# Attention maxima 22 steps ahead instead of 24, and the softmax shift sent in rows instead of half rows

## The chip, the cores and the metric

The kernel runs on one core of one Trainium2 chip. A core has five engines with a queue of their own each: TensorE (PE in the profile; its weight loads stand as PEld), VectorE (DVE), ScalarE (ACT), GpSimd (POOL), and SyncE (SP), which here only issues transfers. They meet through semaphores. The metric is the device time of one execution in microseconds; lower is better.

## The reference

One transformer block with conditioned layer norms, on 2048 tokens of width 512:

```python
mod = silu(c) @ w_mod                       # 512 -> 6 x 512: sa, ca, ga, sb, cb, gb
h = layernorm(x) * (1 + ca) + sa
# A: attention, 32 heads of 16
q, k, v = split(h @ wqkv)
p = softmax(q @ k.T * 16 ** -0.5)           # 2048 x 2048 for each head
x = x + ga * ((p @ v) @ wo)
h = layernorm(x) * (1 + cb) + sb
# B: spatial shift, then an MLP 512 -> 1792 -> 512
x1 = h + shifted(gelu(layernorm(h) @ w1)) @ w2
x = x + gb * (x1 + gelu(layernorm(x1) @ w3) @ w4)
```

All inputs are float32. The weights are scaled up (by 8 in attention, by 64 in B), so the scores reach far and the softmax needs its maximum taken off.

## The kernel before, in words

**Precision.** A float32 product is made of three TensorE products of parts (a high and a low part on each side). For the scores this is folded into the contraction: each of the 16 dimensions of a head takes three rows, so queries and keys of a head stand in 48 of 64 rows. Two heads lie in one tile, head j = 0 in partitions 0 to 63 and j = 1 in 64 to 127; TensorE works on both halves at the same time.

**Units and steps.** Attention is cut into 64 units: 4 chunks of 512 queries times 16 pairs of heads. A unit has 16 steps, one for each 128 keys, 1024 steps in all. In a step each of the two heads has

- a score product (`sc`, L1009): 128 keys x 512 queries into one of seven shared PSUM banks; the weights are a block of the keys `kst`, the streamed operand is the query tile `qtl`;
- an exponential on ScalarE (`pt<-sc`, L1005), written as a 32-bit integer; its upper half is used as a 16-bit number as it stands, the lower half after one halving (`pt<-pt`), which the planner puts on GpSimd (L1058) or, where GpSimd is behind, on ScalarE (L153 in the profile, the same operation);
- value products (`pv`, L1083 for the upper and L1080 for the lower halves).

**The maximum.** A softmax shift for each query is needed before the first score of its unit. It is found by a second product with the roles turned (`mb`, L993): the weights are 128 queries out of 512, the streamed operand 512 keys. VectorE takes the maximum along the keys (`mx<-mb`, L989). A unit needs 4 query groups x 4 key chunks x 2 heads = 32 such products, as many as it has scores. They run `LEAD` steps ahead: beside the scores of step s stand the maxima products of step s + LEAD. Before the first score lie LEAD steps with maxima alone, and in the last LEAD steps there are scores alone.

**The shift.** When a unit's last maximum is in, `max_fin` makes from it a high and a low part in `nm` (two small ScalarE operations L1040 and L1041, one on GpSimd L1042), one value for each query: queries lie along the partitions there. They must become two rows of the query tile (rows 62 and 63 of each head's half, against rows of ones in the keys), so that the score product itself subtracts them. `shift_rows` does that with transfers from SBUF to SBUF on SP's queue: one for each head, part and half of the 512 queries, eight in a unit, each of 128 pieces of 8 bytes (two neighbouring queries from one partition). The first score of the unit waits for them. A group of 128 queries must therefore be the queries that lie in one column of `nm`: groups 0 and 1 are the even and odd queries of the first 256, groups 2 and 3 those of the last 256, and the maxima product's weights are read from the query tile with a step of two.

**Loads.** Keys and queries of a unit come from DRAM by four transfers (`load_unit`) into one of three buffers, issued 32 steps ahead of its first score, when the unit three before has ended.

**The order of work.** A planner (`Sched`) writes all queues at build time from modelled durations: it keeps a clock for each engine and places operations of chains when their engine is modelled free. The attention loop goes in blocks of three rows (a row is one head's score and the other head's maxima product, which use different halves of TensorE), then the value products of an earlier block. Between blocks the generators' work is filled in: the projections of q, k and v during the first units, the beginning of the tail (`tail(0)`: wo, w1) during the last 30 steps. After attention the tail runs for the last 500 us, most of it products L356, L358, L360.

Of the kernel before, what the change touches and what calls it, by code (L numbers as in the profile page):

```python
# [8 lines left out]
F32 = mybir.dt.float32  # L9
# [25 lines left out]
VMAX = 2.0 ** 14  # L35
VD = 20

LEAD = 24
LAG = 2
CARRY = 3000.0  # L40
BMAX = 1600.0
# [286 lines left out]
def kernel(ctx, tc, A_x, A_wqkv, A_wo, B_w1, B_w2, B_w3, B_w4, c, w_mod, out):  # L328
    nc = tc.nc
    te, act, dve, pool, dma = nc.tensor, nc.scalar, nc.vector, nc.gpsimd, nc.sync  # L330
# [21 lines left out]
    def mark(key):  # L352
        return None, 0, lambda: done.add(key)
# [64 lines left out]
    sch = Sched()  # L418
# [535 lines left out]
    qst, vst, mxs = {}, {}, {}  # L954
# [18 lines left out]
    def bank(nm):  # L973
        x = sm.take()
        return x, ap_.tile([P, CH], F32, name=nm, tag=f"s{x}", bufs=1)

    def max_part(m, j):

        u, i = divmod(m, 16)
        c, g = divmod(i, 4)  # L980
        if u not in mxs:
            mxs[u] = at.tile([P, 2, 4, NC], F32, name="mx", tag="mx", bufs=2)
        x, b = bank("mb")
        ready, sm.t[x] = sm.t[x], LATE
        r = slice(64 * j, 64 * j + 62)
        lhs = qst[u][r, (g // 2) * 256:(g // 2 + 1) * 256].rearrange("p (n l) -> p l n", l=2)[:, g % 2]

        def after(e):
            end = sch.crit("D", 605, e + PX, lambda: dve.reduce_max(mxs[u][:, j, g, c:c + 1], b, axis=AX.X))  # L989
            sm.t[x] = end + XP["D"]  # L990
            if (c, g, j) == (NC - 1, 3, 0):
                max_fin(u)
        return ready, lambda: te.matmul(b, lhs, kst[u % 3][r, c * CH:(c + 1) * CH], start=True, stop=True), after  # L993

    def score_part(s, j):

        u, kt = divmod(s, NKT)
        if j == 0:
            pt[s] = at.tile([P, 2, CH], I32, name="pt", tag="pt", bufs=NPT)
        x, b = bank("sc")  # L1000
        ready, sm.t[x] = sm.t[x], LATE
        r = slice(64 * j, 64 * j + 64)

        def after(e):
            ea = sch.crit("A", 480, e + PX, lambda: act.activation(pt[s][:, j], b, AF.Exp))  # L1005
            sm.t[x] = ea + XP["A"]
            if j:
                e_exp[s] = e_hi[s] = ea
        return ready, lambda: te.matmul(b, kst[u % 3][r, kt * P:(kt + 1) * P], qst[u][r], start=True, stop=True), after  # L1009

    def row_pair(s, j):

        parts = []
        if 0 <= s < NS:
            parts.append((j, score_part(s, j)))
        if s + LEAD < NS:
            parts.append((1 - j, max_part(s + LEAD, 1 - j)))
        parts = [x for _, x in sorted(parts, key=lambda x: x[0])]

        def mms():  # L1020
            for _, mm, _ in parts:
                mm()
        e = sch.put("P", CROW, max(x[0] for x in parts), mms)
        return [partial(x[2], e) for x in parts]

    def max_fin(u):
        mf = at.tile([P, 8], F32, name="mf", tag="mf", bufs=2)
        nm = at.tile([P, 2, 8], F32R, name="nm", tag="nm", bufs=2)
        mx = mxs.pop(u)

        def shift_rows():
            for j in range(2):
                for i in range(2):
                    r = 64 * j + 62 + i
                    for h in range(2):
                        sch.dma(dma.dma_start,
                                qst[u][r:r + 1, h * 256:(h + 1) * 256].bitcast(F32).rearrange("o (p l) -> o p l", l=2),
                                nm[:, i, 4 * j + 2 * h:4 * j + 2 * h + 2].bitcast(F32))
        sch.chain(("D", 85, lambda: dve.reduce_max(mf.rearrange("p (j g) -> p j g", j=2), mx, axis=AX.X)),
                  ("A", 100, lambda: act.activation(mf, mf, AF.Copy, scale=-1.0, bias=PEXP)),  # L1040
                  ("A", 100, lambda: act.activation(nm[:, 0], mf, AF.Copy)),  # L1041
                  ("G", 250, lambda: pool.tensor_tensor(nm[:, 1], mf, nm[:, 0], op=OP.subtract)),  # L1042
                  (None, 0, shift_rows), mark(("shift", u)), prio=0, ready=sch.T["D"])
# [550 lines left out]

    blocks = [list(range(i, min(i + GRP, 2 * NS))) for i in range(-2 * LEAD, 2 * NS, GRP)]
    pvs = [x for s in range(0, NS, 2) for x in ((s, 0), (s + 1, 0), (s, 1))]
    due = 0.0
    for k, blk in enumerate(blocks + [[]] * (LAG + CPER)):
# [18 lines left out]
        t, start = CIN, 0.0  # L1617
        need = sum((s >= 0) + (s + LEAD < NS) for s, _ in row)
        sch.flush(need)
        banks = sorted(sm.t)  # L1620
        n = 0
        for s, i in row:
            n += (s >= 0) + (s + LEAD < NS)

# [102 lines left out]
```

## Time and profile before

| what | us |
|---|---|
| median of 3 runs (lowest to highest) | 2027.61 (2023.54 to 2027.86) |
| the profiled execution | 2030.02 |
| its span, first to last instruction | 2028.2 |
| PE busy / PEld busy | 1941.1 / 1168.8 |
| DVE busy / ACT busy / POOL busy | 1658.8 / 1511.4 / 1569.9 |
| maxima alone (first maxima product to first score) | 95.5 to 130.4 |
| scores and maxima together | 130.4 to 1488.4 |
| scores alone | 1488.4 to 1528.9 |

The profiled execution is 2.4 us above the median of the runs shown, and 1.8 us of it lie outside the span. An engine's busy time is the union of its instructions. On TensorE the ends are modelled, and the shown time of a product includes its weight load where that was not hidden: 0.50 us against 0.39. In a timeline row, "x2 0.30" are two overlapping instructions of one kind that together took 0.30 us; the brackets behind a row give the idle time ahead of it and what ended it. The chain is the sequence of work that ended last, followed back through whoever released each step.

### The profile page before, as it was taken

What the parts mean: (1) busy time and instruction counts of PE and PEld (TensorE: products, weight loads), DVE (VectorE), ACT (ScalarE), POOL (GpSimd) and SP (SyncE); (2) the same over time, 40 slices, a digit from 0 to 9 for tenths busy, and PEclk for the clock granted to TensorE, in tenths of its full rate; (3) what the DMA queues carried; (4) which work ended last, traced back from release to release, by engine and by line L of the source; (5) the groups of instructions that cost most, each with busy time, mean ns of one, the idle gap of its engine ahead of it and who ended that gap; (6) DMA issues with size and microseconds to landing.
All of it is one profiled execution on the core that took longest, in us unless ns stands there. A gap on an engine that the chain in (4) does not pass through costs nothing.

```text
span 2028.2 us, 41674 instructions
## 1 busy us (share of the span) xinstructions
PE 1941.1 (96%) x14456; PEld 1168.8 (58%) x14456; DVE 1658.8 (82%) x2979; ACT 1511.4 (75%) x3085; POOL 1569.9 (77%) x1488
## 2 busy tenths in 40 slices
PE   8999999999999999999999999999998889999999
PEld 5755554554444444444444444444447778898998
DVE  6398788879999999999999999999965786556443
ACT  6438887768999989999999999999984554344443
POOL 6349998879999999999999999999994554335222
PEclk9989999999999999999999999999999899999999
DMA  8877666544443435353434343454414677553541
GB/s 302 233 203 183 158 190 165 135 126 118 81 97 81 97 72 106 72 107 72 107 72 98 80 102 76 95 162 93 90 38 146 228 261 274 218 201 122 200 154 68
DMA packets 185508, 278.01 MB, mean 137 GB/s; under 512 B 117104, under 2 KB 127856, under 8 KB 169008
## 3 DMA queue, kind: packets, MB, share of 16 engines
q1 hardware_dynamic: 181792, 267.20, 49.0%
q10 hardware_dynamic: 2304, 4.20, 0.6%
q0 software_dynamic: 1200, 3.93, 0.5%
q8 instruction: 115, 1.88, 0.4%
q14 instruction: 97, 0.79, 0.1%
HBM read 211.81 MB, written 62.91 MB: 135 GB/s over the span
## 4 chain that ended last, share of the span: by engine, by line
PE 61%; DVE 16%; ACT 10%; issue 6%; POOL 4%; DMA 3%; SPq 1%; ACTq 0%; POOLq 0%; DVEq 0%
PE mb L993 13%; DVE mx L989 11%; PE pv L1083 9%; PE sc L1009 8%; ACT pt L1005 7%; PE w L360 6%; PE w L356 6%; PE w L358 6%; PE pv L1080 4%; PE ot L1110 3%; POOL pt L1058 2%; PE xT L1244 1%; DMA wr<-Ws 1%; DMA wst<-in_A_wqkv_dram 1%; SPq L132 1%
## 5 line engine op out<-in xcount | busy, mean ns | idle before, releaser
L989 DVE TENSOR_REDUCE mx<-mb 128x1 f32<-128x512 f32 x2048 | 1250.1, 680 | 74.5 <-PE mb L993 68.6
L1058 POOL TENSOR_SCALAR pt<-pt 128x1024 f16<-128x1024 uint16 x953 | 1248.1, 1365 | 78.7 <-ACT pt L1005 75.7
L1005 ACT ACTIVATE pt<-sc 128x512 int32<-128x512 f32 x2048 | 1061.3, 615 | 125.6 <-PE mb L993 98.0
L993 PE MATMUL mb<-kst,qtl 62*128 62x512 f32 x2048 | 782.7, 462 | 19.9 <-ACT pt L1005 9.9
L1009 PE MATMUL sc<-qtl,kst 64*128 64x512 f32 x2048 | 739.7, 449 | 5.0 <-DVE mx L989 2.5
L993 PEld LDWEIGHTS mb<-kst,qtl 62*128 62x128 f32 x2048 | 360.1, 193 | 232.3 <-ACT pt L1005 159.9
L1009 PEld LDWEIGHTS sc<-qtl,kst 64*128 64x128 f32 x2048 | 337.0, 186 | 186.8 <-DVE mx L989 119.3
L1083 PE MATMUL pv<-pt,vst 128*32 128x512 f16 x4096 | 385.3, 397 | 20.5 <-ACT ac L1100 20.5
L1456 POOL TENSOR_TENSOR g<-sq,g 128x256 fp32r<-128x256 f32 (+1 forms) x124 | 97.2, 787 | 200.6 <-ACT g L1455 187.2
L1080 PE MATMUL pv<-pt,vst 128*32 128x512 f16 (+1 forms) x2048 | 220.8, 389 | 2.5 <-POOL pt L1058 2.4
L1083 PEld LDWEIGHTS <-vst 128*32 128x32 bf16 x4096 | 91.8, 93 | 227.7 <-issue 209.2
L358 PE MATMUL w<-A,wr 128*128 128x256 f32 (+1 forms) x520 | 156.1, 300 | 0.3 <-DVE A L346 0.3
L356 PE MATMUL w<-A,wr 128*128 128x256 f32 (+1 forms) x520 | 155.9, 300 | 0.2 <-ACT A L350 0.2
L360 PE MATMUL w<-A,wr 128*128 128x256 f32 (+1 forms) x520 | 155.8, 300 | 0.0
L1452 ACT ACTIVATE sq<-w 128x256 f32<-128x256 f32 (+1 forms) x130 | 52.3, 402 | 136.0 <-PE w L360 127.2
L356 PE MATMUL w<-wr,g 128*128 128x512 f32 x270 | 106.9, 396 | 2.9 <-DMA wr<-Ws 2.9
L360 PE MATMUL w<-wr,g 128*128 128x512 f32 x270 | 106.5, 394 | 0.9 <-POOL g L1456 0.9
L358 PE MATMUL w<-wr,g 128*128 128x512 f32 x270 | 106.1, 393 | 0.0
L1434 DVE SCALAR_TENSOR_TENSOR sq<-sq,w 128x256 f32<-128x256 f32 (+1 forms) x130 | 58.3, 449 | 57.7 <-ACT sq L1454 57.5
L356 PEld LDWEIGHTS w<-A,wr 128*128 128x128 f32 x520 | 101.7, 196 | 1.6 <-ACT A L350 0.5
L358 PEld LDWEIGHTS w<-A,wr 128*128 128x128 f32 x520 | 101.5, 195 | 1.5 <-DVE A L346 0.5
L360 PEld LDWEIGHTS w<-A,wr 128*128 128x128 f32 x520 | 101.3, 195 | 0.5 <-issue 0.5
(156 smaller groups left out, 2128.5 us busy)
## 6 DMA issues: line engine op xcount, KB each, us to landing
wr<-Ws SPq DMA_DIRECT2D x66, 1024.0 KB, 5.5
vst<-Vs SPq DMA_DIRECT2D x64, 768.0 KB, 5.6
kst<-Ks SPq DMA_DIRECT2D x126, 384.0 KB, 6.2
Ws<-wr SPq DMA_DIRECT2D x14, 1024.0 KB, 6.2
qtl<-Qs SPq DMA_DIRECT2D x128, 96.0 KB, 4.3
Vs<-vt SPq DMA_DIRECT2D x32, 384.0 KB, 4.2
Ks<-qk SPq DMA_DIRECT2D x16, 512.0 KB, 4.2
Qs<-qk SPq DMA_DIRECT2D x16, 512.0 KB, 3.0
```

What stands on the lines that cost most here:

```text
L356: te.matmul(o, lh, rh, start=first, stop=False)
L358: te.matmul(o, lh, rl, start=False, stop=False)
L360: te.matmul(o, ll, rh, start=False, stop=last)
L989: end = sch.crit("D", 605, e + PX, lambda: dve.reduce_max(mxs[u][:, j, g, c:c + 1], b, axis=AX.X))
L993: return ready, lambda: te.matmul(b, lhs, kst[u % 3][r, c * CH:(c + 1) * CH], start=True, stop=True), after
L1005: ea = sch.crit("A", 480, e + PX, lambda: act.activation(pt[s][:, j], b, AF.Exp))
L1009: return ready, lambda: te.matmul(b, kst[u % 3][r, kt * P:(kt + 1) * P], qst[u][r], start=True, stop=True), after
L1058: e_low[s] = XP["G"] + sch.crit("G", 1345, ready, lambda: pool.tensor_scalar(o, i, 0.5, 1.0, op0=OP.mult, op1=OP.mult))
L1080: te.matmul(acc[r:r + n, :], v[:, kt + i, c:c + n].bitcast(F16), pt[s + i].bitcast(F16)[:, j, 0::2], start=False, stop=kt == NKT - 2, skip ...
L1083: te.matmul(acc[r:r + 32, :], v[:, kt, r:r + 32], pt[s].bitcast(F16)[:, j, 1::2], start=kt == 0, stop=False, skip_group_check=True)
L1110: te.matmul(b[:, t * n:(t + 1) * n], ac[:, t * P:(t + 1) * P], smat.rearrange("p j d -> p (j d)"), start=True, stop=True)
L1456: ("G", cG(n), lambda: pool.tensor_tensor(lo, sq, hi, op=OP.subtract)), (None, 0, end), bank=b)
```

## The change

`LEAD` goes from 24 to 22. The shift's rows go in one transfer each, four in a unit instead of eight, each of 128 pieces of 16 bytes (four neighbouring queries from one partition). The groups of queries follow: group g is now every fourth query from g on, and the maxima product's weights are read from the query tile with a step of four, 16 bytes, instead of two.

```diff
-LEAD = 24
+LEAD = 22
@@ max_part
         r = slice(64 * j, 64 * j + 62)
-        lhs = qst[u][r, (g // 2) * 256:(g // 2 + 1) * 256].rearrange("p (n l) -> p l n", l=2)[:, g % 2]
+        lhs = qst[u][r, :].rearrange("p (n l) -> p l n", l=4)[:, g]
@@ max_fin, shift_rows
             for j in range(2):
                 for i in range(2):
                     r = 64 * j + 62 + i
-                    for h in range(2):
-                        sch.dma(dma.dma_start,
-                                qst[u][r:r + 1, h * 256:(h + 1) * 256].bitcast(F32).rearrange("o (p l) -> o p l", l=2),
-                                nm[:, i, 4 * j + 2 * h:4 * j + 2 * h + 2].bitcast(F32))
+                    sch.dma(dma.dma_start, qst[u][r:r + 1, :].bitcast(F32).rearrange("o (p l) -> o p l", l=4),
+                            nm[:, i, 4 * j:4 * j + 4].bitcast(F32))
```

Since the planner writes the queues, LEAD moves more than the maxima. No instruction is added but for the transfers, of which there are 256 instead of 512. Of the halvings of `pt`, 82 instead of 71 stand on ScalarE and 942 instead of 953 on GpSimd. Of the projections' products, 64 instead of 72 stand between the first maxima product and the first score, and 14 of the tail's (3 of wo, 11 of w1) that stood among the last scores now stand behind the last one.

On TensorE, around the program's first score (`mb` maxima products, `sc` scores, `q` and `vb` projection work; the numbers behind `kst` and `qtl` tell buffers apart), the queue before reads:

```order
L993 MATMUL mb<-kst_967,qtl_965 128x512 x3
L356 MATMUL q<-hT_118,wp 128x512
L358 MATMUL q<-hT_118,wp 128x512
L360 MATMUL q<-hT_118,wp 128x512
L356 MATMUL q<-hT_118,wp 128x512
L358 MATMUL q<-hT_118,wp 128x512
L1009 MATMUL sc<-qtl_145,kst_147 128x512
L993 MATMUL mb<-kst_967,qtl_965 128x512 x2
L1009 MATMUL sc<-qtl_145,kst_147 128x512 x2
L993 MATMUL mb<-kst_967,qtl_965 128x512
```

The same place in the changed program:

```order
L803 MATMUL vb<-wab,gcol 128x256
L993 MATMUL mb<-kst_967,qtl_965 128x512 x3
L803 MATMUL vb<-wab,gcol 128x256 x3
L993 MATMUL mb<-kst_967,qtl_965 128x512 x5
L1009 MATMUL sc<-qtl_145,kst_147 128x512
L993 MATMUL mb<-kst_967,qtl_965 128x512
L356 MATMUL q<-hT_118,wp 128x512
L358 MATMUL q<-hT_118,wp 128x512
L360 MATMUL q<-hT_118,wp 128x512
```

The first score comes four maxima products earlier, inside a block of three rows instead of at its start, and the q products that stood ahead of it now follow.

On ScalarE, around the shift of the unit 46 (`mf` and `nm` are the shift, `pt<-sc` the exponentials, L153 a halving, L1100 the copy at the end of a unit), before:

```order
L1005 ACTIVATE pt<-sc 128x512 x6
L153 ACTIVATE pt<-pt 128x1024
L1005 ACTIVATE pt<-sc 128x512 x3
L1040 ACTIVATE mf<-mf 128x8
L1041 ACTIVATE nm<-mf 128x8
L1005 ACTIVATE pt<-sc 128x512 x21
L153 ACTIVATE pt<-pt 128x1024
L1100 ACTIVATE ac<-pv 128x512
```

In the changed program (its line numbers are two lower from here on):

```order
L1005 ACTIVATE pt<-sc 128x512 x6
L153 ACTIVATE pt<-pt 128x1024
L1005 ACTIVATE pt<-sc 128x512 x3
L1038 ACTIVATE mf<-mf 128x8
L1039 ACTIVATE nm<-mf 128x8
L1005 ACTIVATE pt<-sc 128x512 x18
L1098 ACTIVATE ac<-pv 128x512
L1005 ACTIVATE pt<-sc 128x512 x3
L153 ACTIVATE pt<-pt 128x1024
```

Of the exponentials behind `nm`, 12 belonged to the unit at work before the first one of the unit 46 came; now 8 do. Over the attention's regular part it is 12 to 14 before and 7 to 10 now: the shift is made two steps, four scores, nearer to its use.

## The prediction

> **What bounds the kernel now.** I read the page first: span, busy times and the chain.
>
> ```profile
> span 2028.2 us, 41674 instructions
> PE 1941.1 (96%) x14456; PEld 1168.8 (58%) x14456; DVE 1658.8 (82%) x2979; ACT 1511.4 (75%) x3085; POOL 1569.9 (77%) x1488
> PE mb L993 13%; DVE mx L989 11%; PE pv L1083 9%; PE sc L1009 8%; ACT pt L1005 7%; PE w L360 6%; PE w L356 6%; PE w L358 6%; PE pv L1080 4%; PE ot L1110 3%; POOL pt L1058 2%; PE xT L1244 1%; DMA wr<-Ws 1%; DMA wst<-in_A_wqkv_dram 1%; SPq L132 1%
> ```
>
> PE seems to bound all, but a modelled busy time says little, and the costliest single entries of the chain are the maxima products and their reductions, the work the change touches. So I cut the span into stages with the windows view (us, then busy and count of PE, PEld, DVE, ACT, POOL, then granted clock): maxima alone, projections beside attention, regular attention, scores alone. The same view, for the reductions of L989 alone, counts the steps.
>
> ```profile
> 95.00:130.00 35.00, 33.49 (x123) 19.91 (x124) 33.60 (x59) 5.33 (x12) 9.22 (x8) 0.90 0.68 169
> 130.00:500.00 370.00, 359.06 (x2768) 191.67 (x2767) 313.21 (x535) 296.78 (x613) 329.48 (x281) 0.99 0.63 162
> 500.00:1488.00 988.00, 955.85 (x8119) 453.58 (x8118) 944.41 (x1642) 909.92 (x1803) 942.56 (x805) 0.99 0.43 91
> 1488.00:1529.00 41.00, 38.82 (x275) 20.17 (x273) 19.00 (x38) 29.25 (x59) 39.82 (x43) 1.00 0.26 74
> ...
> 500.00:1488.00 988.00, 937.90 (x1543) 0.99 0.43 91
> ```
>
> Maxima alone are bound by DVE (33.6 of 35), scores alone by POOL (39.8 of 41). In the long regular stage, half the span, PE, DVE and POOL are all at 95 to 97%: nothing there is spare by more than 5%. Two reductions a step give 988 / (1543 / 2) = 1.28 us a step.
>
> Where three engines are level, the chain tells which one a small extra lands on. I took it for 25 regular us (share by line; then the first and the last of the 15 pieces that start with an exposed weight load, those of 0.42 us and more; 10 of the 15 are `mb`, 5 are `sc`):
>
> ```profile
> by line: PE mb L993 26.8%; ACT pt L1005 20.1%; PE pv L1083 18.3%; PE sc L1009 16.0%; issue 8.7%; PE pv L1080 6.4%; PE ot L1110 4.0%; ACT mf L1040 0.9%; ACT pt L153 0.5%; ACTq L1041 0.3%; ACT nm L1041 0.1%; ACTq L1005 0.0%
> ...
> 1126.11 0.49 PE mb L993
> 1126.61 0.23 PE sc L1009
> ...
> 1149.07 0.74 PE mb L993 x2
> ```
>
> A product behind another takes 0.23 us, one behind a wait 0.42 to 0.50, since its weight load then stands in the path.
>
> **The change part by part. First, the weights with a step of four.** It adds no instruction; it changes how 2048 loads walk through the query tile. These are their groups, then one block of three rows in the order of time:
>
> ```profile
> L993 PEld LDWEIGHTS mb<-kst,qtl 62*128 62x128 f32 x2048 | 360.1, 193 | 232.3 <-ACT pt L1005 159.9 <-DVE mx L989 40.3 <-issue 5.0
> L1009 PEld LDWEIGHTS sc<-qtl,kst 64*128 64x128 f32 x2048 | 337.0, 186 | 186.8 <-DVE mx L989 119.3 <-ACT pt L1005 32.5 <-issue 12.0
> ...
> L993 PEld LDWEIGHTS mb<-kst,qtl x2048: 189/191/335, 95.5 to 1488.4; 62*128 62x128 f32 x187
> ...
> 1128.31 0.18 PEld L1009 LDWEIGHTS sc<-qtl,kst 64*128 64x128 f32 x1 [0.45 <-DVE mx L989]
> 1128.31 0.30 PEld L993 LDWEIGHTS mb<-kst,qtl 62*128 62x128 f32 x2
> 1128.43 0.41 PEld L1009 LDWEIGHTS sc<-qtl,kst 64*128 64x128 f32 x2
> ```
>
> Two loads that overlap take 0.30 us, one alone 0.19, so the pass over 128 weights takes 0.11 and the rest is latency. In that pass an `sc` load (contiguous) walks over 128 x 4 = 512 bytes of each partition, an `mb` load (step two) over 1024 bytes, that is 9.3 bytes per ns. A streamed operand of 512 contiguous numbers, 2048 bytes in 0.23 us, goes at 8.9. No row of this trace goes faster. With a step of four the load walks over 2048 bytes; at the same pace it takes 0.22 us, 0.11 more. The bounds: nothing, since the step from one to two, 186 to 193 ns, shows no kink; and 335 - 191 = 0.14, the longest load seen. I take 0.11, because the streamed operand is the nearest row in bytes walked and it stands at the limit.
>
> The Trainium skill says on this ("SBUF — State Buffer", Specifications (TRN2)) that a 16-byte line of SBUF has to be hit at least twice for full bandwidth. Two hits, the step of two, run at full pace here, as it says; one hit no run here shows, and the page gives no figure for it; by it the load costs more, as taken.
>
> What lies on the path: loads of the second and third row of a block are issued while the products ahead still stream, and 0.22 still fits under 0.23, so these cost nothing; if a load took longer than 0.23, that cover would be gone for all 2048. The exposed ones are the first of each run of rows. In the 25 us above, 26.8% and 16.0% are 10.7 us with 10 exposed `mb` loads. Over the span the chain has 13% and 8%, 426 us, so 426 / 10.7 x 10 = 398 exposed `mb` loads: 398 x 0.11 = 44 us. Upper end: the 5 of 15 that start with `sc` are slowed as well, since the `mb` beside them starts later and the rows end together: 597 x 0.14 = 84 us. Lower end: 0. The other engines cover little: at 95% busy they are 44 us short of filling the stage themselves. Queued behind a slow load are the block's scores and value products; VectorE and ScalarE wait for them.
>
> **Second, LEAD 22.** Two steps of maxima alone go: -2 x 35.0 / 24 = -2.9 us. Two steps more have both: +2 x 1.28 = +2.6. Two steps of scores alone go: -2 x 41.0 / 24 = -3.4. But those ends were also filled with other products, and the queues in order show where they went: 8 q products into the projection stage (PE 359 of 370) and 14 of the tail behind the last score. At the 0.23 us of a 512-wide product (the 11 of w1 are 256 wide, half of that) it is 8 x 0.23 + 3 x 0.23 + 11 x 0.12 = 3.8 us that come back. Sum 0.1. Counted by PE alone, the program has four rows fewer, -4 x 0.23 = -0.9, and one or two changes between rows and value products. I take -1, with -4 (the moved products find holes) and +4 as ends.
>
> **Third, the shift in four transfers.** The rows for all transfers of it, and for the unit 46:
>
> ```profile
> L132 SPq DMA_DIRECT2D qtl<-nm x512: 468/593/1826, 121.3 to 1496.7; - x171
> ...
> DMA to landing us min/median/max: 1.9/2.0/5.9
> ...
> qtl<-Qs SPq DMA_DIRECT2D x128, 96.0 KB, 4.3
> ...
> 1140.90 5.29 SPq L132 DMA_DIRECT2D qtl<-nm  x8
> 1147.61 0.31 SPq L132 DMA_DIRECT2D qtl<-Qs  x1
> ...
> 1147.08 0.50 PE L1009 MATMUL sc<-qtl,kst 64*128 64x512 f32 x1
> 1147.43 0.61 PE L1009 MATMUL sc<-qtl,kst 64*128 64x512 f32 x2
> ```
>
> Today there is almost nothing to spare: the eighth issue starts at about 1140.90 + 5.29 - 0.60 = 1145.6 and lands 1.9 us later, at 1147.5; the scores that need it start at 1147.08 (first head) and 1147.43. The shift is now made 2 x 1.28 = 2.56 us nearer to the scores. Four issues fewer, 5.29 / 2, give 2.6 back. An issue costs by its pieces, 128 before and after, and not by bytes: the query load in the same rows moves 96 KB, in 48 long pieces, with a 0.31 us issue. So 0, as good as exact; the lower end is 0, since PE hardly waits for it now, the upper one issue of the longest kind (1826 - 593 = 1.2 us) in every third of 63 units: 25 us. Behind the shift on SP stand the loads of the next unit; they are first used two steps later than now, so they gain room.
>
> **Fourth, 11 halvings from POOL to ACT.** 1.37 us each on either (POOL 1.365 in its group, 1.37 the one at 1137.75 on ACT), 15 us off POOL's 943 and onto ACT's 910 of 988: both have room, cost 0, ends -2 and +2.
>
> ```profile
> L1058 POOL TENSOR_SCALAR pt<-pt 128x1024 f16<-128x1024 uint16 x953 | 1248.1, 1365 | 78.7 <-ACT pt L1005 75.7
> 1137.75 1.37 ACT L153 ACTIVATE pt<-pt 128x1024 f16<-128x1024 uint16 x1
> ```
>
> **Sum.** 2030.0 (the profiled execution) + 44 - 1 + 0 + 0 = 2073; against the median, 2.4 lower, 2070.6, so 2070 us.
>
> **The rivals.**
> - The load isn't dearer, and the rest cancels: 2027.6 - 1, within 4 us, so 2027. For it speaks that 186 to 193 shows no kink. It decides whether the `mb` load's mean stays near 193. The same page of the Trainium skill, in its section on the DMA port swizzle, also says that fp32 can be stepped over by four for free; that reading gives this time.
> - Faster: the load isn't dearer, and the moved products fall into holes of PE. In the stage of scores alone, whose chain is POOL's at 65%, two steps less shorten POOL's own queue and one halving of 1.4 us there moves to ACT: -2.9 + 2.6 - 3.4 - 1.4 = -5.1, so 2022.5. It decides from the point where less than 1 us of the 3.8 comes back.
>
> ```profile
> by line: POOL pt L1058 64.8%; POOL trs L1353 8.3%; issue 7.5%; DVE A L346 3.1%; DVE mx L989 2.9%; POOL trs L1357 2.3%; ACT A L350 1.5%; POOL trs L1358 1.4%; PE w L356 1.2%; PE w L358 1.1%; PE wo L356 1.0%; PE sc L1009 1.0%; PE pv L1080 1.0%
> ```
>
> - The shift lands late, the load is not dearer: `nm` waits behind halvings on ACT and POOL (the one at 1137.75 stands just ahead of it), and with two steps less a wait of 0.5 us at each of 62 units gives +31: 2058. Against it: the halved number of issues.
> - The load takes more than the 0.23 us that cover it, say 0.33: then each of 2048 rows takes 0.1 more, +205, less what PE idles before such loads and could give (232 and 187 us in the groups, mostly while it waits for its own consumers): some +150, 2180. Nothing in the trace shows so slow a load.
>
> **How the numbers follow.** Forecast 0.53, no change 0.14, faster 0.18, late shift 0.10, uncovered load 0.05. What a measurement here can tell from no change is about 0.2%, 4 us. Slower by more: 0.53 + 0.10 + 0.05 = 0.68; within: 0.14; faster: 0.18. The forecast's own range is 2040 to 2095: half the exposed loads at 0.06, up to 600 at 0.11. The range for all reaches from the middle of the faster case, 2021, to 2096; it leaves out the uncovered load, half of the faster case and the forecast's far end.
>
> **What would show it.** The `mb` weight loads at about 300 ns instead of 193, those of `sc` still at 186; the first `mb` product of a block at 0.60 instead of 0.50; a step of 1.33 us or more in the regular stage, DVE and POOL below 93% there, and more of the chain on `mb`. Of the shift: 256 issues of some 0.59 us, landing in 2.0, no wait of `sc` for them beyond today's. The stage of maxima alone near 32 us. The prediction is wrong if the loads stay near 193, or if they rise and the regular stage doesn't lengthen, which would mean that exposed loads were hidden by the waits for DVE and ACT that they follow.

## The result and the profile after

| | before | changed |
|---|---|---|
| median, us | 2026.4 (2023.54 to 2027.86, 4 runs) | 2056.5 (2053.49 to 2057.77, 4 runs) |
| ratio, 95% interval | | 1.0146 (1.0133 to 1.016) |
| profiled execution / its span | 2030.02 / 2028.2 | 2053.49 / 2051.7 |

The changed kernel is slower by 1.46%, some 30 us; the profiled spans differ by 23.5 us, since the profiled execution of the changed kernel is the fastest of its four and that of before (2030.02) lies above the four listed here. The page of the changed kernel, span, engines and chain, and last the chain by engine of before:

```profile
span 2051.7 us, 41094 instructions
PE 1996.3 (97%) x14456; PEld 1314.7 (64%) x14456; DVE 1663.5 (81%) x2979; ACT 1526.0 (74%) x3096; POOL 1560.1 (76%) x1477
PE 82%; DVE 8%; ACT 4%; issue 2%; POOL 1%; DMA 1%; ACTq 0%; SPq 0%; DVEq 0%; POOLq 0%
PE mb L993 20%; PE sc L1009 14%; PE pv L1081 14%; PE pv L1078 6%; PE w L360 5%; PE w L358 5%; PE w L356 5%; DVE mx L989 4%; PE ot L1108 3%; ACT pt L1005 3%; PE xT L1242 1%; PE q L356 1%; DVE tst L367 1%; PE v L356 1%; PE q L360 1%
...
PE 61%; DVE 16%; ACT 10%; issue 6%; POOL 4%; DMA 3%; SPq 1%; ACTq 0%; POOLq 0%; DVEq 0%
```

The chain went over to PE: 82% of the span instead of 61%, the maxima products `mb` 20% instead of 13%, VectorE 8% instead of 16%. PE is busy 55 us longer (1941.1 before), on the same products. The groups say which (the first line is the group of `mb` products before), and one block in the order of time shows how (weight loads first, then the products; the number ahead of the engine is the duration):

```profile
L993 PE MATMUL mb<-kst,qtl 62*128 62x512 f32 x2048 | 782.7, 462 | 19.9 <-ACT pt L1005 9.9
...
L993 PE MATMUL mb<-kst,qtl 62*128 62x512 f32 x2048 | 846.9, 521 | 9.3 <-ACT pt L1005 4.9
L993 PEld LDWEIGHTS mb<-kst,qtl 62*128 62x128 f32 x2048 | 520.1, 307 | 177.0 <-ACT pt L1005 120.5
L1009 PEld LDWEIGHTS sc<-qtl,kst 64*128 64x128 f32 x2048 | 369.0, 191 | 160.6 <-DVE mx L989 107.4
...
1125.01 0.31 PEld L993 LDWEIGHTS mb<-kst,qtl 62*128 62x128 f32 x1 [0.45 <-ACT pt L1005]
1125.01 0.18 PEld L1009 LDWEIGHTS sc<-qtl,kst 64*128 64x128 f32 x1
...
1125.01 0.62 PE L993 MATMUL mb<-kst,qtl 62*128 62x512 f32 x1
1125.01 0.50 PE L1009 MATMUL sc<-qtl,kst 64*128 64x512 f32 x1
1125.35 0.40 PE L993 MATMUL mb<-kst,qtl 62*128 62x512 f32 x1
```

The `mb` load takes 307 ns instead of 193; the `sc` load is unchanged at the head of a block (0.18), its mean goes from 186 to 191. The first `mb` product of the block takes 0.62 us instead of 0.50, the next, whose load ran under it, 0.40.

Where in the span the time went, I read from stages whose edges are the first scores of units 0, 16 and 60 and the end of the last score. In the regular part, units 16 to 59 (windows view: us, PE, PEld, DVE, ACT, POOL), before and after:

```profile
533.90:1435.70 901.80, 872.48 (x7398) 413.03 (x7395) 861.89 (x1499) 831.16 (x1645) 860.97 (x735) 0.99 0.44 93
```

```profile
553.10:1460.40 907.30, 904.08 (x7394) 510.06 (x7390) 864.59 (x1496) 839.39 (x1651) 852.27 (x726) 1.00 0.41 92
```

PE's busy time rises by 31.6 us there and its idle time falls from 29.3 to 3.2: the stage is only 5.5 us longer, and PE has nothing left in it. The other stages: up to the first score 126.8 instead of 130.4 us (-3.6); units 0 to 15 426.3 instead of 403.5 (+22.8); from unit 60 to the last score 92.9 instead of 93.7; the tail 498.4 instead of 498.8. The sum is the 23.5 us, nearly all of it in units 0 to 15, where the projections run.

The shift arrives in time, as its transfers show (tile `nm`: duration min, median, max in ns; then who waited):

```profile
L132 SPq DMA_DIRECT2D qtl<-nm x256: 468/588/1560, 121.7 to 1523.3; - x128
...
who waited for it (us, times):
  POOL nm L1040: 15.3, 12
  PE sc L1009: 0.6, 2
```

### The profile page after: what moved, and what is told of

It reads as the page before. It is cut to its first block, busy times and chain, and to the rows that moved or that the text cites. A ratio compares the mean times of both kernels' runs of the same rounds, so it can differ in the third digit from the quotient of the medians.

```text
span 2051.7 us, 41094 instructions
## 1 busy us (share of the span) xinstructions
PE 1996.3 (97%) x14456; PEld 1314.7 (64%) x14456; DVE 1663.5 (81%) x2979; ACT 1526.0 (74%) x3096; POOL 1560.1 (76%) x1477
## 4 chain that ended last, share of the span: by engine, by line
PE 82%; DVE 8%; ACT 4%; issue 2%; POOL 1%; DMA 1%; ACTq 0%; SPq 0%; DVEq 0%; POOLq 0%
PE mb L993 20%; PE sc L1009 14%; PE pv L1081 14%; PE pv L1078 6%; PE w L360 5%; PE w L358 5%; PE w L356 5%; DVE mx L989 4%; PE ot L1108 3%; ACT pt L1005 3%; PE xT L1242 1%; PE q L356 1%; DVE tst L367 1%; PE v L356 1%; PE q L360 1%
## 5 line engine op out<-in xcount | busy, mean ns | idle before, releaser
L993 PE MATMUL mb<-kst,qtl 62*128 62x512 f32 x2048 | 846.9, 521 | 9.3 <-ACT pt L1005 4.9
L993 PEld LDWEIGHTS mb<-kst,qtl 62*128 62x128 f32 x2048 | 520.1, 307 | 177.0 <-ACT pt L1005 120.5
L1009 PEld LDWEIGHTS sc<-qtl,kst 64*128 64x128 f32 x2048 | 369.0, 191 | 160.6 <-DVE mx L989 107.4
L153 ACT ACTIVATE pt<-pt 128x1024 f16<-128x1024 uint16 x82 | 114.0, 1390 | 0.0
L356 PEld LDWEIGHTS w<-A,wr 128*128 128x128 f32 x520 | 101.4, 195 | 1.1 <-ACT A L350 0.2
L358 PEld LDWEIGHTS w<-A,wr 128*128 128x128 f32 x520 | 101.0, 194 | 1.4 <-DVE A L346 0.4
```

The source lines that it names most:

```text
L153: fn()
L356: te.matmul(o, lh, rh, start=first, stop=False)
L358: te.matmul(o, lh, rl, start=False, stop=False)
```

## The experiments

Three theories stand against each other: the slower weight load costs the time; the new order (LEAD and what it moves) does; the shift lands late.

**One part alone: the step of four.** The kernel before, with eight transfers; each puts its pairs where the new grouping wants them.

```diff
@@ max_part
-        lhs = qst[u][r, (g // 2) * 256:(g // 2 + 1) * 256].rearrange("p (n l) -> p l n", l=2)[:, g % 2]
+        lhs = qst[u][r, :].rearrange("p (n l) -> p l n", l=4)[:, g]
@@ shift_rows
-                                qst[u][r:r + 1, h * 256:(h + 1) * 256].bitcast(F32).rearrange("o (p l) -> o p l", l=2),
+                                qst[u][r:r + 1, :].bitcast(F32).rearrange("o (p a l) -> o p a l", a=2, l=2)[:, :, h],
```

> LEAD 24 and eight transfers as before; only the maxima weights are read with a step of four, and each transfer's pieces land where that grouping wants them. Theory of the weight load: the whole loss is here, the mb load at 306 ns as in the changed kernel and a ratio to before of 1.012 to 1.018. Theory of the order (LEAD and the new queues cost the time): the load rises too, but the ratio stays within 1.003. Theory of a late shift: as the theory of the order, since the shift has its old lead here.

Measured: 2058.19 us, ratio 1.0153 (1.0134 to 1.0173). The weight load alone makes the whole loss. `mb` products take 521 ns in the mean, as in the changed kernel.

```profile
PE 1986.1 (97%) x14456; PEld 1314.7 (64%) x14456; DVE 1661.7 (81%) x2979; ACT 1515.4 (74%) x3085; POOL 1572.9 (76%) x1488
...
L993 PEld LDWEIGHTS mb<-kst,qtl 62*128 62x128 f32 x2048 | 520.0, 307 | 175.8 <-ACT pt L1005 126.4 <-DVE mx L989 23.3 <-issue 7.1
```

PE is busy 45.0 us longer than before; the span, 2057.5 us, is 29.3 longer; PE's idle time (span less busy) falls from 87.1 to 71.4. By stages: units 0 to 15 +10.4 us, units 16 to 59 +18.8, the rest +0.1.

**The changed kernel with the old LEAD.**

```diff
-LEAD = 22
+LEAD = 24
```

> The changed kernel with LEAD back at 24: step of four, four transfers. Theory of the weight load: 1.012 to 1.018 against before, within 0.3% of the changed kernel, since LEAD is worth -1 us and at most 4. Theory of the order: near 1.000. Theory of a late shift: under 1.005, the shift now having 2.5 us to spare.

Measured: 2060.28 us, ratio 1.0165 (1.0139 to 1.019). LEAD doesn't cost the time, and with four transfers the loss is the same as with the eight of the first experiment. Whether it brings some can't be told from these intervals. Its small sum hides larger parts. Against this kernel's profile (first score at 130.6, units 0 to 15 414.4 us, units 16 to 59 918.8), the changed one's stages are -3.8, +11.9 and -11.5.

**LEAD alone: the kernel before with 22, the shift in eight transfers.**

```diff
-LEAD = 24
+LEAD = 22
```

> LEAD 22 alone: step of two and eight transfers as before. By the reckoning of the shift, it is made 2.56 us nearer to its score and nothing is saved at its transfers, with 0.1 to 0.6 us to spare before: some 2 to 2.5 us late at each of about 47 regular units, so +90 to +120 us if PE's wait goes through, ratio 1.04 to 1.06, and waits of sc for the transfers of nm of that size in the profile. Rival: the other engines catch up behind the wait or the planner's order hides it, under 1.01.

Measured: 2132.13 us, ratio 1.0514 (1.049 to 1.0539). The wait is there, first line of PE's waits, and the page's chain by engine and by line:

```profile
PE sc L1009 <- DMA qtl<-nm: 66.2, 55, 1.9
...
PE 57%; ACT 8%; DVE 8%; SPq 7%; issue 7%; POOL 6%; DMA 6%; ACTq 0%; POOLq 0%; DVEq 0%
PE mb L993 10%; PE sc L1009 9%; PE pv L1083 8%; SPq L132 7%; ACT pt L1005 6%; PE w L360 5%; PE w L356 5%; PE w L358 5%; POOL pt L1058 5%; DMA qtl<-nm 5%; DVE mx L989 4%; PE pv L1080 3%; PE ot L1110 2%; PE xT L1244 1%; PE q L356 1%
```

55 waits of up to 1.9 us; the transfers and SP's issuing of them hold 12% of the chain (7 for SP, its other issues on that line among them, and 5 for the transfers), where before only SP's 1% appears. But the waits make 66.2 us, 1.2 us each, and not the whole 104. Over the span PE's idle time grows by 54.7 us and its busy time by 48.4, with the granted clock at 0.966 instead of 0.987. Units 16 to 59 and, below, a stretch 0.9 us behind the end of one such wait (in the last columns the granted clock, DMA share and GB/s):

```profile
548.70:1534.50 985.80, 913.06 (x7394) 420.86 (x7393) 869.99 (x1497) 845.05 (x1651) 856.84 (x726) 0.95 0.40 85
...
619.90:623.30 3.40, 3.40 (x22) 1.67 (x16) 1.89 (x3) 1.73 (x4) 2.31 (x3) 0.50 1.14 202
```

The stage is 84.0 us longer than before and PE is busy 40.6 us longer in it on the same products, at a clock of 0.95 instead of 0.99. The trace has 24 stretches at half the clock there, 88.7 us together; before has 2, 10.2 us. Half of the difference, an estimate, is 39 us. Of the 24 stretches 22 begin during a wait for the shift or within 2 us after it; that the waits bring the lower clock is likely from this, but no run takes the two apart. So two steps of lead are worth 100 us with eight transfers, waits and clock together, and the change can only take them away because it halves the transfers at the same time.

**Half the loads.** In the kernel before, the step of four for the first head of each pair alone.

```diff
@@ max_part
+        if j == 0:
+            lhs = qst[u][r, :].rearrange("p (n l) -> p l n", l=4)[:, g]
+        else:
             lhs = qst[u][r, (g // 2) * 256:(g // 2 + 1) * 256].rearrange("p (n l) -> p l n", l=2)[:, g % 2]
@@ shift_rows
-                                qst[u][r:r + 1, h * 256:(h + 1) * 256].bitcast(F32).rearrange("o (p l) -> o p l", l=2),
+                                (qst[u][r:r + 1, :].bitcast(F32).rearrange("o (p a l) -> o p a l", a=2, l=2)[:, :, h] if j == 0 else qst[u][r:r + 1, h * 256:(h + 1) * 256].bitcast(F32).rearrange("o (p l) -> o p l", l=2)),
```

> As before, but the step of four for the first head's maxima products alone, 1024 of 2048 loads. Theory of exposed loads that add up: half the loss of the full step, ratio 1.006 to 1.009. Rival, a loss only where the slow load is the last thing the block waits for: far from half, under 1.003 or near the full 1.014.

Measured: 2047.15 us, ratio 1.0102 (1.0081 to 1.0123): 18.5 us of the full step's 29.5. That is between half and two thirds, above the 1.006 to 1.009 that was expected, though the intervals still allow the half. Neither form of the rival (under 1.003, or near the full loss) holds.

**VectorE as the bound.** Two of a unit's 32 reductions are done twice (the result is the same), first in the kernel before, then in that of the first experiment.

```diff
-            end = sch.crit("D", 605, e + PX, lambda: dve.reduce_max(mxs[u][:, j, g, c:c + 1], b, axis=AX.X))
+            def maxima():
+                for _ in range(1 + (g == 0 and j == 0 and c < 2)):
+                    dve.reduce_max(mxs[u][:, j, g, c:c + 1], b, axis=AX.X)
+            end = sch.crit("D", 605 * (1 + (g == 0 and j == 0 and c < 2)), e + PX, maxima)
```

> The kernel before, with 2 of a unit's 32 reductions done twice (the planner knows of it): 1.2 us more for VectorE in a unit of 20.3 us, 77 us over the span, which puts VectorE above the 96% it has in the regular stage. No theory of the change says anything of this run alone; it is the base for the next one. Expected ratio to before 1.02 to 1.04.

> The same doubled reductions with the step of four (eight transfers, LEAD 24). Theory that the other engines' waits take in a part of the slower loads: with VectorE the bound there is more to take it in, and the step of four costs under 15 us over the run before it in this list, instead of 29.5. Rival, an exposed load adds its time wherever it stands: again 25 to 35 us.

Measured: 2075.12 us (1.0229, 1.0209 to 1.0249) and 2101.9 us (1.0362, 1.0338 to 1.0385). The step of four costs 26.8 us here, against 29.5 without the doubled reductions: my theory, that the other engines' waits take in a part, falls. Step of two and of four, engines and chain from the pages, then VectorE's waits for maxima products (us in total, times, longest):

```profile
PE 1978.1 (95%) x14456; PEld 1185.4 (57%) x14456; DVE 1740.3 (84%) x3107; ACT 1504.0 (73%) x3069; POOL 1588.8 (77%) x1504
DVE 49%; PE 39%; DMA 3%; ACT 3%; issue 3%; POOL 2%; SPq 1%; POOLq 0%; DVEq 0%; ACTq 0%
...
DVE mx L991 <- PE mb L996: 35.0, 47, 2.8
```

```profile
PE 2027.5 (96%) x14456; PEld 1323.0 (63%) x14456; DVE 1742.7 (83%) x3107; ACT 1506.1 (72%) x3069; POOL 1591.5 (76%) x1504
PE 61%; DVE 25%; DMA 3%; POOL 3%; ACT 3%; issue 3%; SPq 1%; ACTq 0%; POOLq 0%; DVEq 0%
...
DVE mx L991 <- PE mb L996: 61.1, 104, 2.3
```

PE's busy time rises by 49.4 us, the spans (2072.3 and 2102.0) by 29.7, and PE's idle time falls by 19.7. A share of VectorE of 49% in the chain was no cover: VectorE waits for the same slow products, 61.1 us instead of 35.0. The run also tests the way in which the prediction counted. The chain of the step of two has only 145 `mb` pieces with an exposed load (of 0.42 us and more), so counted as in the prediction the step of four should have cost 145 x 0.11 = 16 us here; it cost 26.8.

**The load by its step.** In the kernel before, 12 products for each of eight steps at the end of the program, one loop like the one shown for each of s = 1, 2, 3, 4, 5, 6, 8 and 16; nothing reads their values but one reduction into an unused column (`lw` and `lr` are 62 partitions of two buffers of the tail).

```diff
 (kernel before, after the tail)
+        for _ in range(12):
+            te.matmul(lad, lw[:, 0:128 * s].rearrange("p (n l) -> p l n", l=s)[:, 0], lr, start=True, stop=True)
```

> The kernel before, with 96 products of 62 rows x 128 weights x 512 columns at its end, 12 for each of the steps 1, 2, 3, 4, 5, 6, 8 and 16 in the weights; only their load times matter. By a pace of 9.3 bytes walked per ns, as I argued: 183 to 191 ns at steps 1 and 2, 245 at 3, 300 at 4, 355 at 5, 410 at 6, 520 at 8, and 960 at 16, with products following each other at 0.23 us up to step 4 and at the load's pass beyond. By the rule of two hits on a 16-byte line: a rise between 2 and 4 and the same 306 from step 4 on, products at 0.23 us throughout.

Measured (min/median/max in ns, first and last start; steps 1, 2, 3, 4, 5, 6, 8, 16 from above):

```profile
L1700 PEld LDWEIGHTS lad<-A,g x12: 182/184/186, 2021.8 to 2024.2; 62*128 62x128 f32 x12
...
L1702 PEld LDWEIGHTS lad<-A,g x12: 190/190/191, 2024.4 to 2027.0; 62*128 62x128 f32 x12
...
L1704 PEld LDWEIGHTS lad<-A,g x12: 248/249/250, 2027.2 to 2029.8; 62*128 62x128 f32 x12
...
L1706 PEld LDWEIGHTS lad<-A,g x12: 305/306/308, 2030.0 to 2032.6; 62*128 62x128 f32 x12
...
L1708 PEld LDWEIGHTS lad<-A,g x12: 293/296/308, 2032.9 to 2035.5; 62*128 62x128 f32 x12
...
L1710 PEld LDWEIGHTS lad<-A,g x12: 299/303/304, 2035.7 to 2038.3; 62*128 62x128 f32 x12
...
L1712 PEld LDWEIGHTS lad<-A,g x12: 318/326/327, 2038.5 to 2041.2; 62*128 62x128 f32 x12
...
L1714 PEld LDWEIGHTS lad<-A,g x12: 295/296/307, 2041.5 to 2044.1; 62*128 62x128 f32 x12
```

The load rises from step 2 to step 4 and then stays. A pace of bytes walked falls: 16 numbers apart costs no more than 4. A count of 16-byte lines fits: steps 1, 2, 3 and 4 touch 32, 64, 96 and 128 lines, and any larger step 128; from 64 lines on, 32 lines more cost 58 ns. A price for each line that is hit only once fits as well: with a step of three half of the weights stand alone in their line, and the load lies half way. Twelve loads start 0.22 to 0.25 us apart at every step, so the slow load still fits about under its product. (This run's time has the added products in it and says nothing else.)

**What gave time back in the regular part?** With the step of four, units 16 to 59 take 920.6 us with LEAD 24 and 907.3 in the changed kernel. Five runs looked for the reason. First, in the kernel before, another LEAD with which the blocks of three rows lie in a unit as with 22:

```diff
-LEAD = 24
+LEAD = 25
```

> The kernel before with LEAD 25: step of two, eight transfers, 76 halvings on ACT. From the first score of unit 16 to that of unit 60 the kernel before takes 901.8 us, the changed one 907.3, but the one with the step of four alone 920.6: with LEAD 22 something gave 13 us back there. Theory of the blocks: 2 x 22 and 2 x 25 leave the same rest by three, so the blocks of three rows lie the same way in a unit, and this stretch falls by some 13 us, to about 889. Theory of the halvings (82 instead of 71 on ACT did it): no fall beyond 4 us. In either case the shift has 1.3 us more to spare, which brings nothing, since PE waited 1.4 us for it in all.

Measured: 2031.08 us, ratio 1.0023 (1.0012 to 1.0034), units 16 to 59 899.4 us against 901.8. Not the blocks, as far as the step of two shows; with the step of four this was not run. Then more halvings on ScalarE, in the kernel before and in that of the first experiment:

```diff
-LACT = 200.0
+LACT = 0.0
```

> The kernel before with the planner's threshold for the halvings at 0 instead of 200 ns: 89 instead of 71 of them on ACT, 935 on POOL, all else by the same rules. Theory of the halvings: the stretch from unit 16 to unit 60 falls from 901.8 by 5 to 15 us. Theory of the blocks: it stays within 4 us.

> The step of four with eight transfers and LEAD 24, and the threshold at 0: 89 halvings on ACT. Theory of the halvings: the stretch from unit 16 to unit 60 falls from 920.6 to about 907, as in the changed kernel, the ratio to before from 1.015 to about 1.009. Theory of the blocks: both stay.

Measured: 2054.54 us (1.0134, 1.0119 to 1.0149) and 2082.0 us (1.0266, 1.0246 to 1.0287); units 16 to 59 take 921.7 and 938.5 us, more and not less. Not the halvings' number. Last, in the same two kernels, their place: where a unit's value products end, no halving may stand ahead of the copy of the accumulator.

```diff
-    def p_low(s):
+    def p_low(s, hold):
...
-        if g > a + LACT:
+        if g > a + LACT and not hold:
...
+        hold = any(s % NKT == NKT - 2 and i for s, i in col)
         for s in low:
-            p_low(s)
+            p_low(s, hold)
```

> The kernel before, with no halving put on ACT in a block that ends a unit's value products. In before the copy of the finished accumulator (L1100) stands right behind a halving on ACT in 17 of 64 units, in the changed kernel in 3, and PE's waits of value products for that copy are 20.5 us in the one and 2.6 in the other. Theory that this wait is what LEAD 22 removed by chance: here the wait falls under 4 us, the stretch from unit 16 to unit 60 from 901.8 by 8 to 15, and the ratio to before is 0.993 to 0.996, faster than both. Rival, the wait only took the place of another one: stretch and ratio as before, within 0.2%.

> The same rule on ACT with the step of four (eight transfers, LEAD 24). Theory of the copy's wait: the stretch from unit 16 to unit 60 falls from 920.6 to some 907, as in the changed kernel, and the ratio from 1.015 to about 1.009. Rival: both stay.

Measured: 2040.09 us (1.0071, 1.0052 to 1.0089) and 2062.0 us (1.018, 1.0161 to 1.02). PE's waits for the copy, in before, in the changed kernel and with this rule:

```profile
PE pv L1083 <- ACT ac L1100: 20.5, 19, 1.2
```

```profile
PE pv L1081 <- ACT ac L1098: 2.6, 4, 1.5
```

```profile
PE pv L1083 <- ACT ac L1100: 3.4, 10, 0.5
...
536.20:1447.20 911.00, 897.70 (x7398) 421.35 (x7396) 861.50 (x1498) 828.66 (x1645) 862.48 (x735) 1.00 0.43 92
```

The wait goes, but the stretch becomes longer, 911.0 us, with PE busy 897.7 instead of 872.5 on the same products; with the step of four it is 923.2 us instead of 920.6. The durations of the stretch's products add up to the same in both kernels with the step of two, 3051 and 3054 us, so they overlap less; what makes them do so isn't shown. So this theory falls too. By the count, the first experiment's waits for the copy, 18.1 us against 2.6, are about what the changed kernel's regular part lacks, but removing them elsewhere brought nothing. Why LEAD 22 is rid of them and faster there, and why it pays with 12 us in the projection stage, stays open. No version here is faster than the kernel before.

## Why the prediction came out right

- **Direction and cause: right.** Slower was forecast, 2070 us within 2021 to 2096, measured 2056.5; the cause, the weight load with a step of four, is shown by itself in the first experiment. That the loss would lie in the regular stage was not right for the changed kernel: units 16 to 59 hold 5.5 us of it and units 0 to 15 22.8. In the first experiment it is 18.8 and 10.4.
- **Price of a load: right, for a partly wrong reason.** Forecast 0.11 us more, about 300 ns; measured 307 against 193. The argument by bytes walked gives the right values up to step four (245 and 300 where the ladder has 249 and 306) and fails behind it, where the ladder is flat (296 at step 16, not 960). A cost by lines of 16 bytes fits all eight steps roughly. The Trainium skill ("SBUF — State Buffer", Specifications (TRN2)) asks for two hits on a line. The traces agree that two hits cost almost nothing (190 against 184) and that one hit costs more (306); the value between (249 at a step of three, where some lines are hit once and some twice) excludes only a switch for the load as a whole. The Trainium skill's other reading (same page, in its section on the DMA port swizzle), that fp32 may be stepped over by four for free, the ladder refutes: a step of four is already at the full price.
- **What lies on the path: the step that was mis-sized.** "398 x 0.11 = 44 us" was the term; the first experiment measured 29.5 for it (29.3 in the spans). One part is the count, which was scaled up from 25 us: the whole chain of the kernel before has 339 such `mb` pieces, which at 0.114 us make 39. The rest is the reckoning itself, which let each exposed load on the chain lengthen the program by its full price. The chain's count is no bound either way: it gave too much here and too little with the doubled reductions (16 against 26.8).
- **The 45.0 us by which PE's busy time grew in the first experiment are near the 44 by luck.** They don't come from 398 loads: the mean `mb` product grew by 59 ns where its load grew by 114, so about half of the 2048 loads pass their extra on to their product, and many of these products run beside a score product. By the account of the trace PE's idle time, 87.1 us before, fell by 15.7 (31.7 in the changed kernel), so the span grew by less than the busy time. This is an account and not yet a cause: the rule on the copy's place alone made PE busy 25 us longer on the same products. Which exposed loads cost time, and which don't, stays open.
- **Hidden loads: right in part.** "These cost nothing" was said of the second and third rows of a block. From before to the first experiment, in units 16 to 59, the first `mb` product of a block grew by 114 ns (507 to 621), the second by 25 and the third by 34. In before, 301 of the 469 third products there took 0.42 us or more already, the prediction's own mark of an exposed load.
- **LEAD: -1 us, right as a sum within the noise,** and as a story too simple: against the changed kernel with LEAD 24 it is -3.8 us to the first score (forecast -2.9), but then +12 in the projection stage and -12 in the regular one.
- **The shift: 0, right.** Its balance of 2.56 us nearer against 2.6 us saved held with 0.6 us of PE's waits in all. Its counterpart, LEAD 22 with eight transfers, cost 104 us where the expectation gave 90 to 120, in part by luck: the waits are 1.2 us each and not 2 to 2.5, and the lower clock made up the rest. The rival of a late shift, 2058, lies nearer to the measured 2056.5 than the forecast does, but only by its number: its waits of 0.5 us a unit did not come, and the load, which it took as unchanged, is the cause.
- **Signs:** loads near 300, first product near 0.60, chain to `mb`, maxima alone near 32 us (31.4) came as told. The regular step came to 1.30 us, not 1.33 (1509 reductions in 980 us), and VectorE stayed at 95% there and GpSimd at 93.5, not below 93, since the loss was smaller and for the greater part in the first units.

## What to carry to other kernels

A change that adds no instruction can still make one dearer: four-byte weights read one in 16 bytes load 1.6 times as long here, and where such a load stands behind a wait its extra can go into the path. The chain's count of exposed loads gives the sign and the order of size of such an extra, not more: 44 forecast for 29.5 here, and 16 for 26.8 in the kernel whose chain lay half on VectorE. A run with that part alone is what settles it. The bounds of other engines are no cover when they wait for the same instruction. A lead time and the number of transfers inside it belong together: shortened together they cost nothing measurable, the lead alone 100 us, about half of it as longer busy time of PE at a lower granted clock.

## What the runs showed that I had not expected

- The weight load's cost is flat from a step of four to one of 16 (306, 296, 303, 326, 296 ns) and at a step of three it lies half way (249).
- With VectorE at half of the chain, the slower loads on TensorE cost as much (26.8 us) as without (29.5).
- Around waits of TensorE of 1 to 2 us the granted clock fell to half for 3.4 us, in two cases 6.8: 24 such stretches in units 16 to 59 of the kernel with LEAD 22 alone, 22 of them within such a wait or just behind it, against 2 in the kernel before.
- An order that takes away most of a 20 us wait of TensorE for ScalarE made the kernel 0.7% slower, and moving 18 more halvings from GpSimd to ScalarE, both with room in their busy times, made it 1.3% slower. In this stage, where four engines stand above 90%, the order of the queues mattered more than these shares.
